# Diagonals from unnormalised taps spread in fp32r, division at the evacuation, and x rows loaded and transposed block by block

## The chip, the cores and the metric

One core of one Trainium2 chip. The metric is the device time of one execution in microseconds, lower is better. The span of a profile is the same execution seen by the profiler, about 1.7 us shorter than the device time.

## The reference, cut to what matters

```python
# x: (8, 4096, 192), weight: (8 heads, 7 taps)
w = softmax(weight, axis=-1)                        # taps of each head
y[b, s, h] = sum_k w[h, k] * x[b, s + k - 6, h]     # causal convolution, zero padded
h = y.reshape(32768, 192) @ w_in                    # w_in: (192, 2048)
g = h * sigmoid(beta * h)                           # beta: one value per column
out = g @ w_out                                     # w_out: (2048, 192), fp32 result
```

## The kernel before

The kernel works on steps of up to 512 tokens of two batch halves at once. One step is 16 units: a unit does six `hidden` matmuls, one ScalarE activation (`Silu(beta*h)`; the factor 1/beta is put into w_out), and the `output` matmuls of the step before. In the steady state VectorE makes the convolved input `ct` two steps ahead, by 21 multiply and multiply-add operations on a transposed `xt`.

The start is different. Step 0 (256 tokens) and step 1 (256 tokens) have no time for that, so TensorE does their convolution with diagonal matrices in fp32r, a cheaper form of fp32 for matmuls (three fp32 matmuls of the taps show as six records in the trace, three fp32r ones as three). The copy of a matmul's result out of PSUM, TensorE's result memory, is called its evacuation. Step 2 is the first whose `ct` VectorE makes. The parts that matter, with cuts:

```python
# w_in chunk 0 is the first load that POOL issues, then sel and ident are built
load_w_in(0)
...                                     # sel (memset, two affine_selects), ident
load_x(nc.gpsimd, x1b, TOK, 0, NB)      # second chunk of x, cast to bf16
for i in range(1, NW): load_w_in(i)
for c in range(0, NF, 4):               # w_out last, four loads
    nc.gpsimd.dma_start(out=w_out_raw[:, c:c+4, :], in_=w_out_v[:, c:c+4, :])
...
nc.scalar.activation(cw8, cw8, AF.Exp, bias=nmax, accum_out=ssum)
nc.vector.reciprocal(rsum, ssum)
nc.vector.tensor_scalar_mul(cw8, cw8, rsum)
fill(6)                                 # matmuls of zeros
for c in range(NG):                     # fp32 spread of the taps to 128 partitions
    nc.tensor.matmul(pc[:, 0, c*K:(c+1)*K], sel[:, c], cw8, start=True, stop=True)
...
transposes(pt, x0b, 0, 0, HB)           # first half of chunk 0
fill(2)
diag_v(1); ...                          # diagonals = ident * taps, fp32r
diag_conv(0, 1, ...)                    # 7 matmuls, then ct by VectorE
diag_conv(0, 2, ...)
transposes(ptb, x0b, HB, 0, HB)         # second half of chunk 0
diag_conv(0, 0, ...)                    # its ct by ScalarE
...
def prep_w_out(c0, n):                  # on POOL, four times, when w_out has landed
    nc.gpsimd.tensor_tensor(w_out_s[:, c0:c0+n, :], w_out_raw[:, c0:c0+n, :],
                            beta_r[:, c0:c0+n].broadcast, ALU.mult)
...
first_work = {                          # extra work inside step 0, by unit
    1: lambda: (more(xt1_work)(), copy_w_in(1)),   # transposes of chunk 1
    3: lambda: (more(xt1_work)(), copy_w_in(2)),
    5: lambda: (more(conv1_work)(), copy_w_in(3)), # taps of step 1, 7 matmuls
    8: more(conv1_work),
    11: more(conv1_work),               # then VectorE evacuates ct of step 1
}
```

`copy_w_in(i)` is a VectorE copy of a w_in chunk from partitions 0-63 to 64-127.

## Time and profile before

| | before |
|---|---|
| device time, median of 3 | 697.0 us (696.14 to 697.85) |
| span of the profile | 695.1 us |
| TensorE busy | 99% |
| first hidden matmul of step 0 | 12.02 us |
| first matmul of step 1 | 25.03 us |
| end of the first hidden group of step 2 | 37.06 us |
| start of the final run of 272 matmuls | 679.63 us |

The last row is a mark near the end: two profiles that differ only in their first 40 us differ at this mark by what the start won or lost.

From the page of the kernel before: the span, busy time by engine, and the chain that ended last.

```profile
span 695.1 us, 24857 instructions
...
PE 686.9 (99%) x11465; PEld 525.9 (76%) x11465; DVE 553.2 (80%) x935; ACT 578.7 (83%) x545; POOL 69.8 (10%) x83
...
PE 96%; DVE 3%; ACT 0%; issue 0%
```

The busy share alone would not prove that TensorE bounds the kernel: the Trainium skill, "Perfetto Trace Analysis", section "Identifying the Most-Contended Engine", says that the matmul busy share is not a good measure of how close a kernel is to roofline, because pipelined TensorE instructions look smaller in the trace. The chain of waits is another road to it, with 96% of the span on TensorE; and after 38 us nothing in the waits view makes TensorE wait longer than 0.2 us. So only the start can move.

The timeline of TensorE at the start (start, duration, engine, line, operation, output<-inputs, shapes, count, and in brackets the idle time before it and what ended it):

```profile
3.94 1.44 PE L208 MATMUL po<-cw_86,sel 8*128 8x7 f32 x6
...
6.87 1.83 PE L249 MATMUL ph<-xt_145,diag 128*128 128x256 f32 x7
...
8.85 1.23 PE L249 MATMUL ph<-xt_145,diag 128*128 128x256 f32 x7
...
10.47 1.09 PE L249 MATMUL po<-xt_145,diag 128*128 128x256 f32 x7
12.02 0.83 PE L363 MATMUL ph<-ct,w_in_s 64*128 64x256 bf16 x12 [0.46 <-ACT ct L261]
...
25.03 0.50 PE L363 MATMUL ph<-ct,w_in_s 64*128 64x256 bf16 x6 [0.54 <-DVE ct L300]
```

The chain of waits from 14 to 37 us (start, duration, what was on it):

```profile
14.88 0.96 DVE xt L314
...
15.87 1.29 DVE w_in_s L149 x2
...
17.18 4.39 DVE ct L344 x3
21.56 2.54 DVE ct L346 x2
24.10 0.87 DVE ct L300
24.97 6.62 DVE ct L346 x10
...
36.67 0.39 PE ph L363 x2
```

After 14.9 us the chain runs on VectorE: the copy of chunk 1's `xt`, two w_in copies, three tap multiplies, two multiply-adds, the evacuation that opens step 1, then the rest of step 2's taps. POOL's w_out multiplications, in POOL's timeline, lie over the middle of it:

```profile
17.00 5.89 POOL L320 TENSOR_TENSOR w_out_s<-w_out_raw,beta_r 128x768 bf16<-128x768 f32 x4 [2.30 <-DMA w_out_raw<-in_moe_w_out_dram]
```

### The profile page before, as it was taken

The page shows a single profiled execution, that of the slowest core. Times are in us where ns is not written, and L with a number is a line of the kernel's source. Part 1 is how long each engine was busy: PE and PEld are TensorE (multiplying, and loading weights), DVE is VectorE, ACT ScalarE, POOL GpSimd, SP SyncE. Part 2 cuts the span into 40 slices and gives each one's busy share as a digit, 9 for nine tenths or more (in the row PEclk, how much of TensorE's full clock was granted, in tenths as well). Part 3 has the DMA queues.
Part 4 walks back from the last instruction along what each step waited for, and adds up shares of the span by engine and source line. Part 5 has one row for each costly group of instructions (what it writes and reads, how often), then busy time and mean ns, then how long its engine had stood idle before and what let it go on. Part 6 is the DMA issues. An engine that isn't in the chain of part 4 may idle for free.

```text
span 695.1 us, 24857 instructions
## 1 busy us (share of the span) xinstructions
PE 686.9 (99%) x11465; PEld 525.9 (76%) x11465; DVE 553.2 (80%) x935; ACT 578.7 (83%) x545; POOL 69.8 (10%) x83
## 2 busy tenths in 40 slices
PE   8899999999999999999999999999999999999997
PEld 6767777777777777777777777777777777777777
DVE  6999999998777987777987777987778987777222
ACT  5898888888888888888888888888888888888881
POOL 6934455000000000000000000000000000000000
PEclk9999999999999999999999999999999999999999
DMA  9999999922232022322023222032123122111012
GB/s 175 146 160 160 169 177 171 138 62 70 54 65 71 27 68 72 47 70 70 26 70 71 49 70 69 26 71 70 48 72 55 41 70 71 48 48 48 25 48 70
DMA packets 181497, 54.57 MB, mean 79 GB/s; under 512 B 146432, under 2 KB 181072, under 8 KB 181392
## 3 DMA queue, kind: packets, MB, share of 16 engines
q0 software_dynamic: 98048, 14.89, 29.9%
q1 hardware_dynamic: 83296, 38.09, 23.6%
q8 instruction: 89, 1.46, 0.9%
q14 instruction: 16, 0.13, 0.1%
q10 hardware_dynamic: 48, 0.01, 0.0%
HBM read 28.98 MB, written 37.29 MB: 95 GB/s over the span
## 4 chain that ended last, share of the span: by engine, by line
PE 96%; DVE 3%; ACT 0%; issue 0%
PE po L410 48%; PE ph L363 46%; DVE ct L346 2%; DVE ct L344 1%; PE ph L204 1%; PE ph L249 0%; PE po L236 0%; PE po L208 0%; DVE w_in_s L149 0%; ACT g L370 0%; PE po L249 0%; DVE xt L314 0%; DVE osb L425 0%; DVE ct L300 0%; DVE osb L424 0%
## 5 line engine op out<-in xcount | busy, mean ns | idle before, releaser
L370 ACT ACTIVATE g<-ph,beta 128x1024 bf16<-128x1024 f32 (+1 forms) x528 | 571.8, 1088 | 97.0 <-PE ph L363 93.1
L410 PEld LDWEIGHTS <-g 64*128 64x128 bf16 x8192 | 368.9, 94 | 102.4 <-issue 0.2
L410 PE MATMUL po<-w_out_s,g 64*128 64x192 bf16 x8192 | 429.8, 243 | 0.0
L363 PE MATMUL ph<-ct,w_in_s 64*128 64x512 bf16 (+1 forms) x3168 | 425.5, 370 | 2.8 <-ACT g L370 1.4
L346 DVE SCALAR_TENSOR_TENSOR ct<-xt,cw,ct 128x512 bf16<-128x512 bf16 x558 | 380.4, 746 | 0.0
L363 PEld LDWEIGHTS <-w_in_s 64*128 64x128 bf16 x3168 | 162.4, 94 | 56.9 <-issue 3.6
L424 DVE COPY osb<-po 128x384 f32<-128x384 f32 x127 | 70.8, 558 | 126.3 <-PE po L410 120.2
L425 DVE TENSOR_TENSOR osb<-po,osb 128x384 f32<-128x384 f32 x129 | 71.5, 554 | 6.0 <-ACT osb L422 1.6
L95 POOL DMA_DIRECT2D xd<-in_x_dram x60 | 54.3, 906 | 47.8 <-DMA xd<-in_x_dram 43.5
L344 DVE TENSOR_SCALAR ct<-xt,cw 128x512 bf16<-128x512 bf16 x93 | 31.6, 393 | 0.0
L422 ACT COPY osb<-po 128x192 f32<-128x192 f32 x2 | 0.6, 318 | 9.9 <-PE po L410 9.9
L320 POOL TENSOR_TENSOR w_out_s<-w_out_raw,beta_r 128x768 bf16<-128x768 f32 x4 | 5.9, 1500 | 2.3 <-DMA w_out_raw<-in_moe_w_out_dram 2.3
L204 PE MATMUL ph<-zeros 128*128 128x512 bf16 x8 | 3.8, 627 | 1.3 <-DVE warm L132 1.3
L249 PE MATMUL po<-xt_145,diag 128*128 128x256 f32 x28 | 4.4, 296 | 0.0
L249 PEld LDWEIGHTS po<-xt_145,diag 128*128 128x128 f32 x28 | 3.6, 189 | 0.7 <-issue 0.6
L149 DVE COPY w_in_s<-w_in_s 64x1536 bf16<-64x1536 bf16 x4 | 2.7, 699 | 1.5 <-DMA w_in_s<-in_moe_w_in_dram 1.4
L184 POOL DMA_DIRECT2D w_out_raw<-in_moe_w_out_dram x4 | 3.1, 782 | 0.0
L249 PEld LDWEIGHTS ph<-xt_145,diag 128*128 128x128 f32 x14 | 2.6, 269 | 0.7 <-ACT xt_145 L270 0.6
L249 PE MATMUL ph<-xt_145,diag 128*128 128x256 f32 x14 | 3.1, 375 | 0.0
L204 PEld LDWEIGHTS <-zeros 128*128 128x128 bf16 x8 | 0.9, 130 | 2.5 <-issue 1.3
L142 POOL DMA_DIRECT2D w_in_s<-in_moe_w_in_dram x4 | 2.6, 667 | 0.8 <-POOLq L479 0.8
L261 ACT CAST ct<-po 128x256 bf16<-128x256 f32 x1 | 0.4, 372 | 2.8 <-PE po L249 2.8
(46 smaller groups left out, 27.7 us busy)
## 6 DMA issues: line engine op xcount, KB each, us to landing
out_dram<-osb SPq DMA_DIRECT2D x60, 384.0 KB, 3.0
xd<-in_x_dram POOLq DMA_DIRECT2D x54, 198.0 KB, 14.6
w_out_raw<-in_moe_w_out_dram POOLq DMA_DIRECT2D x4, 384.0 KB, 9.6
out_dram<-osb SPq DMA_DIRECT2D x7, 192.0 KB, 3.8
xd<-in_x_dram POOLq DMA_DIRECT2D x6, 192.0 KB, 14.0
x_83<-in_x_dram SPq DMA_DIRECT2D x4, 192.0 KB, 3.9
w_in_s<-in_moe_w_in_dram POOLq DMA_DIRECT2D x4, 192.0 KB, 7.9
xt<-xd SPq DMA_TRANSPOSE x30, 4.6
```

The source lines that it names most:

```text
L95: nc.gpsimd.dma_start(out=xd[r0:, :, h, :], in_=x_v[p, t0:t1, h, :].rearrange("t (c d) -> t c d", c=NG),)
L184: nc.gpsimd.dma_start(out=w_out_raw[:, c : c + 4, :], in_=w_out_v[:, c : c + 4, :])
L204: nc.tensor.matmul(pf[:, 0, :], zeros[:, 0:128], zeros, start=True, stop=True)
L249: nc.tensor.matmul(pv, diag[:, c, k, :], xt0[:, c, o : o + n], start=(k == 0), stop=(k == K - 1),)
L320: nc.gpsimd.tensor_tensor(w_out_s[:, c0 : c0 + n, :], w_out_raw[:, c0 : c0 + n, :], beta_r[:, c0 : c0 + n].unsqueeze(2).to_broadcast((128, ...
L344: nc.vector.tensor_scalar_mul(dst, src, scalar)
L346: nc.vector.scalar_tensor_tensor(out=dst, in0=src, scalar=scalar, in1=dst, op0=ALU.mult, op1=ALU.add)
L363: nc.tensor.matmul(ph[:, h, 0:n], w_in_s[rows, j, cols], cts[s][rows, j, 0:n], start=(j == 0), stop=(j == NG - 1),)
L370: nc.scalar.activation(gs[s][:, fc, :, 0:n], ph[:, :, 0:n], AF.Silu, scale=beta[:, fc : fc + 1])
L410: nc.tensor.matmul(po[:, r, b * D : (b + 1) * D], g[rows, fc, h, q * BLK : (q + 1) * BLK], w_out_s[rows, fc, :], start=(fc == 0), stop=(fc ...
L424: nc.vector.tensor_copy(dst, po[:, 0, cols])
L425: nc.vector.tensor_tensor(dst, po[:, 1, cols], dst, ALU.add)
```

## The change

The intent is to start the first hidden matmul earlier. The taps are spread as plain exponentials in fp32r, and the division by their sum moves to the evacuation of the convolution. Only VectorE's own taps are still computed exactly, in fp32, but later, inside step 0. The x rows come in one load per block of 128 tokens, so that transposing starts with the first block, and the second half's transposes move into step 0. POOL builds `sel` and `ident` before it issues w_in. The core, with cuts:

```diff
-    load_w_in(0)                       # was first on POOL, now after sel and ident
+    for b in range(nb):                # one load of x per block, both halves
+        eng.dma_start(out=dst[:, b, :, :], in_=x_v[0, t : t + BLK, :, :])
-    nc.scalar.activation(cw8, cw8, AF.Exp, bias=nmax, accum_out=ssum)
-    nc.vector.reciprocal(rsum, ssum)
-    nc.vector.tensor_scalar_mul(cw8, cw8, rsum)
+    nc.scalar.activation(e8[:, 0:K], cw8, AF.Exp, bias=nmax, accum_out=e8[:, K : K + 1])
-    fill(6)
-    (three fp32 matmuls sel x cw8)
+    nc.vector.tensor_copy(sel_r, sel)           # fp32r copies
+    nc.vector.tensor_copy(e8r, e8)
+    fill(5)
+    spread(pc[:, 0, :], sel_r, e8r)             # three fp32r matmuls
+    fill(1)
...
+    for b in range(HB):                         # cast, transpose, evacuate by block
+        nc.vector.tensor_copy(x0b[:, b], x0[:, b])
+        transposes(pt, x0b, b, 0, 1)
+        nc.scalar.copy(xt0[:, :, HALO + b * BLK : HALO + (b + 1) * BLK], pt)
...
-            nc.scalar.copy(ct[:, c, 0 : steps[s][2]], pv)
+            nc.scalar.mul(ct[:, c, 0:n0], pv, rn[:, c : c + 1])   # the division
...
     first_work = {
-        1: lambda: (more(xt1_work)(), copy_w_in(1)),
-        3: lambda: (more(xt1_work)(), copy_w_in(2)),
-        5: lambda: (more(conv1_work)(), copy_w_in(3)),
+        0: lambda: (first_xt(), taps()),  # second half's transposes; fp32 spread
+        2: lambda: (more(xt1_work)(), copy_w_in(1)),
+        4: lambda: (more(xt1_work)(), copy_w_in(2)),
+        6: lambda: (more(conv1_work)(), copy_w_in(3)),
         8: more(conv1_work),
         11: more(conv1_work),
     }
```

More of the change, by code (lines that the diff above doesn't have):

```diff
@@ L113, with load_x @@
     x1b = setup.tile([128, NB, 2, D], BF16)
-    def load_x(eng, dst, t0, b0, nb):
-        for h in range(2):
-            eng.dma_start(
-                out=dst[:, b0 : b0 + nb, h, :],
-                in_=x_v[0, t0 : t0 + nb * BLK, h, :].rearrange(
-                    "(b q) d -> q b d", q=BLK
-                ),
-            )
+    def load_x(eng, dst, t0, nb):
+        for b in range(nb):
+            t = t0 + b * BLK
+            eng.dma_start(out=dst[:, b, :, :], in_=x_v[0, t : t + BLK, :, :])
+    e8 = setup.tile([H, K + 1], FP32)
     cw8 = setup.tile([H, K], FP32)
     nc.scalar.dma_start(out=cw8, in_=weight)
-    load_x(nc.sync, x0, 0, 0, HB)
-    load_x(nc.sync, x0, HB * BLK, HB, HB)
+    load_x(nc.sync, x0, 0, NB)
     zeros = setup.tile([128, TOK], BF16)
@@ L133 @@
     nc.scalar.activation(warm, warm, AF.Exp)
-    NW = 4
-    FW = F // NW
-    w_in_s = consts.tile([128, NG, F], BF16)
-    def load_w_in(i):
-        cols = slice(i * FW, (i + 1) * FW)
-        nc.gpsimd.dma_start(
-            out=w_in_s[0:DG, :, cols],
-            in_=moe_w_in[:, cols].rearrange("(c d) f -> d c f", c=NG),
-        )
-    def copy_w_in(i):
-        cols = slice(i * FW, (i + 1) * FW)
-        nc.vector.tensor_copy(w_in_s[DG : 2 * DG, :, cols], w_in_s[0:DG, :, cols])
-    load_w_in(0)
     sel = setup.tile([H, NG, 2, DG], FP32)
@@ L177, with load_w_in, copy_w_in @@
     make_identity(nc, ident)
+    NW = 4
+    FW = F // NW
+    w_in_s = consts.tile([128, NG, F], BF16)
+    def load_w_in(i):
+        cols = slice(i * FW, (i + 1) * FW)
+        nc.gpsimd.dma_start(
+            out=w_in_s[0:DG, :, cols],
+            in_=moe_w_in[:, cols].rearrange("(c d) f -> d c f", c=NG),
+        )
+    def copy_w_in(i):
+        cols = slice(i * FW, (i + 1) * FW)
+        nc.vector.tensor_copy(w_in_s[DG : 2 * DG, :, cols], w_in_s[0:DG, :, cols])
+    load_w_in(0)
+    for h in range(2):
+        nc.gpsimd.dma_start(
+            out=x1b[:, :, h, :],
+            in_=x_v[0, TOK : 2 * TOK, h, :].rearrange("(b q) d -> q b d", q=BLK),
+        )
+    for i in range(1, NW):
+        load_w_in(i)
     w_out_raw = setup.tile([128, NF, D], FP32)
     w_out_v = moe_w_out.rearrange("(c p) d -> p c d", p=128)
-    load_x(nc.gpsimd, x1b, TOK, 0, NB)
-    for i in range(1, NW):
-        load_w_in(i)
     for c in range(0, NF, 4):
@@ L190 @@
     nc.vector.reduce_max(nmax, cw8, axis=mybir.AxisListType.X, negate=True)
-    ssum = setup.tile([H, 1], FP32)
-    nc.scalar.activation(cw8, cw8, AF.Exp, bias=nmax, accum_out=ssum)
+    nc.scalar.activation(
+        e8[:, 0:K], cw8, AF.Exp, bias=nmax, accum_out=e8[:, K : K + 1]
+    )
     beta_q = setup.tile([NF, 128], FP32)
@@ L195 @@
     nc.scalar.activation(warm, warm, AF.Silu)
-    rsum = setup.tile([H, 1], FP32)
-    nc.vector.reciprocal(rsum, ssum)
-    nc.vector.tensor_scalar_mul(cw8, cw8, rsum)
+    e8r = setup.tile([H, K + 1], FP32R)
+    sel_r = setup.tile([H, NG, 2, DG], FP32R)
     pc = psum_o.tile([128, 2, TOK], FP32, name="po")
@@ L204, in fill, with spread @@
             nc.tensor.matmul(pf[:, 0, :], zeros[:, 0:128], zeros, start=True, stop=True)
-    fill(6)
-    for c in range(NG):
-        nc.tensor.matmul(
-            pc[:, 0, c * K : (c + 1) * K],
-            sel[:, c, :, :].rearrange("i h d -> i (h d)"),
-            cw8,
-            start=True,
-            stop=True,
-        )
+    def spread(dst, sel, e8):
+        for c in range(NG):
+            nc.tensor.matmul(
+                dst[:, c * (K + 1) : (c + 1) * (K + 1)],
+                sel[:, c, :, :].rearrange("i h d -> i (h d)"),
+                e8,
+                start=True,
+                stop=True,
+            )
+    nc.vector.tensor_copy(sel_r, sel)
     ident_b = setup.tile([128, 128], BF16)
     nc.vector.tensor_copy(ident_b, ident)
-    nc.vector.tensor_copy(x0b[:, 0:HB], x0[:, 0:HB])
-    cw = consts.tile([128, NG, K], FP32)
-    nc.vector.tensor_copy(cw.rearrange("p c k -> p (c k)"), pc[:, 0, 0 : NG * K])
+    nc.vector.tensor_copy(e8r, e8)
+    fill(5)
+    spread(pc[:, 0, :], sel_r, e8r)
+    fill(1)
+    eu = setup.tile([128, NG, K + 1], FP32)
+    nc.vector.tensor_copy(eu.rearrange("p c k -> p (c k)"), pc[:, 0, 0 : NG * (K + 1)])
     diag = setup.tile([128, NG, K, 128], FP32R)
@@ L227, in diag_v @@
             ident.unsqueeze(1).to_broadcast((128, K, 128)),
-            cw[:, c, :].unsqueeze(2).to_broadcast((128, K, 128)),
+            eu[:, c, 0:K].unsqueeze(2).to_broadcast((128, K, 128)),
             ALU.mult,
@@ L255, in diag_tap @@
         )
-    def diag_conv(s, c, pv, ct):
-        for k in range(K):
-            diag_tap(s, c, k, pv)
-        if c == 0:
-            nc.scalar.copy(ct[:, c, 0 : steps[s][2]], pv)
-        else:
-            nc.vector.tensor_copy(ct[:, c, 0 : steps[s][2]], pv)
-    n0 = HB * BLK
-    pt = psum_o.tile([128, NG, n0], BF16, name="po")
-    transposes(pt, x0b, 0, 0, HB)
-    fill(2)
+    n0 = HB * BLK
+    for b in range(HB):
+        nc.vector.tensor_copy(x0b[:, b], x0[:, b])
+        pt = psum_o.tile([128, NG, BLK], BF16, name="po")
+        transposes(pt, x0b, b, 0, 1)
+        nc.scalar.copy(xt0[:, :, HALO + b * BLK : HALO + (b + 1) * BLK], pt)
+    fill(1)
+    diag_v(0)
+    rn = setup.tile([128, NG], FP32)
+    nc.vector.reciprocal(rn, eu[:, :, K])
     diag_v(1)
-    nc.scalar.copy(xt0[:, 0:2, HALO : HALO + n0], pt[:, 0:2, :])
-    nc.vector.tensor_copy(xt0[:, 2, HALO : HALO + n0], pt[:, 2, :])
     for k in range(K):
-        nc.scalar.mul(diag[:, 0, k, :], ident, cw[:, 0, k : k + 1])
-    diag_v(2)
+        nc.scalar.mul(diag[:, 2, k, :], ident, eu[:, 2, k : k + 1])
     ct = ct_pool.tile([128, NG, TOK], BF16, name="ct")
     cts[0] = ct
-    diag_conv(0, 1, psum_h.tile([128, 2, TOK], FP32, name="ph")[:, 0, 0:n0], ct)
-    beta_p = pc[:, 0, 32 : 32 + NF]
-    nc.tensor.transpose(beta_p, beta_q, ident[0:NF, 0:NF])
-    beta = consts.tile([128, NF], FP32)
-    nc.vector.tensor_copy(beta, beta_p)
+    pvs = []
+    for c in range(NG):
+        pool, name = (psum_h, "ph") if c < 2 else (psum_o, "po")
+        pv = pool.tile([128, 2, TOK], FP32, name=name)[:, 0, 0:n0]
+        for k in range(K):
+            diag_tap(0, c, k, pv)
+        if c == 0:
+            nc.vector.tensor_scalar_mul(ct[:, c, 0:n0], pv, rn[:, c : c + 1])
+            copy_w_in(0)
+        elif c == 1:
+            nc.vector.tensor_scalar_mul(ct[:, c, 0:n0], pv, rn[:, c : c + 1])
+            pb = psum_o.tile([128, 2, TOK], FP32, name="po")[:, 0, 0:NF]
+            nc.tensor.transpose(pb, beta_q, ident[0:NF, 0:NF])
+            beta = consts.tile([128, NF], FP32)
+            nc.vector.tensor_copy(beta, pb)
+        else:
+            nc.scalar.mul(ct[:, c, 0:n0], pv, rn[:, c : c + 1])
     beta_r = setup.tile([128, NF], FP32)
@@ L284, with taps, first_xt @@
     nc.vector.tensor_copy(x0b[:, HB:NB], x0[:, HB:NB])
-    copy_w_in(0)
-    diag_conv(0, 2, psum_h.tile([128, 2, TOK], FP32, name="ph")[:, 0, 0:n0], ct)
-    ptb = psum_o.tile([128, NG, n0], BF16, name="po")
-    transposes(ptb, x0b, HB, 0, HB)
-    diag_conv(0, 0, psum_o.tile([128, 2, TOK], FP32, name="po")[:, 0, 0:n0], ct)
-    nc.vector.tensor_copy(xt0[:, :, HALO + n0 :], ptb)
+    cw = consts.tile([128, NG, K], FP32)
+    def taps():
+        pq = psum_o.tile([128, 2, TOK], FP32, name="po")[:, 0, 0 : NG * (K + 1)]
+        spread(pq, sel, e8)
+        pq = pq.rearrange("p (c k) -> p c k", c=NG)
+        rq = setup.tile([128, NG], FP32)
+        nc.vector.reciprocal(rq, pq[:, :, K])
+        nc.vector.tensor_tensor(
+            cw, pq[:, :, 0:K], rq.unsqueeze(2).to_broadcast((128, NG, K)), ALU.mult
+        )
+    def first_xt():
+        pt = psum_o.tile([128, NG, n0], BF16, name="po")
+        transposes(pt, x0b, HB, 0, HB)
+        nc.vector.tensor_copy(xt0[:, :, HALO + n0 :], pt)
     def first_conv():
@@ L299, in first_conv @@
             if c == NG - 1:
-                nc.vector.tensor_copy(cts[1][:, :, 0:n0], pv[:, 0:NG, :])
+                nc.vector.tensor_tensor(
+                    cts[1][:, :, 0:n0],
+                    pv[:, 0:NG, :],
+                    rn.unsqueeze(2).to_broadcast((128, NG, n0)),
+                    ALU.mult,
+                )
             yield
```

## The prediction

> **What bounds the kernel now.** TensorE. The page's busy table gives PE 99% of the 695.1 us span. The waits view after 36 us shows one PE wait of 0.3 us on VectorE, so the steady steps (36.7 us to the end) are matmul-bound and the change does not touch them. Only the first 36.7 us can move.
>
> **The start, from the timeline and the chain of waits.** PE: zero fills 1.27-4.0, fp32 spread of the taps 4.01-5.38 (six passes, 355 ns each), transposes to 6.16, two fills to 7.1, first diagonal taps 7.13, three channels until 11.57, ScalarE evacuation 11.59-11.97, first hidden matmul 12.02. Step 0 runs to 24.5. Then PE waits 0.54 us for the first_conv evacuation, step 1 starts at 25.03, and step 2 at 35.75, with a 0.27 us wait for VectorE at 36.67. From 14.9 to 36.7 the chain is almost all VectorE: transposed x 14.88, w_in copies 15.87-17.16, three tap multiplies 17.18-21.56 at 1.46 us each (393 ns average overall), two multiply-adds, evacuation 24.10-24.97, sixteen multiply-adds. The slow multiplies coincide with POOL's four w_out multiplications (17.0-22.9). The Trainium skill, "SBUF — State Buffer", section "Who interferes with whom", says two-port VectorE operations and GpSimd lock each other out; 1.46 against 1.51 us for the POOL operation agrees. POOL itself waits until 17.0 for the w_out load, and VectorE until 13.5 for the second w_in chunk: this middle is paced by DMA.
>
> **Removed, added, moved.**
> - Spread in fp32r: three short passes instead of six; at most 1.37 us becomes about 0.4 (estimate).
> - Normalisation (reciprocal 0.15 + multiply 0.31) leaves the path to the diagonals; but sel_r and e8r copies join it (about 0.45 and 0.1, estimates from copies of like size). sel is ready 0.8 us earlier, since POOL no longer issues w_in first (0.78).
> - Second-half transposes (0.46) and their 0.95 us copy leave the path to the first hidden matmul.
> - First tap about 6.2 instead of 7.13, the last about 10.3 instead of 11.57, first hidden about 10.7 instead of 12.02: 1.3 us earlier.
> - Added inside step 0: those transposes, an fp32 spread (0.7-1.4), the 0.95 us copy, reciprocal and multiply. That returns 1.2-1.9 us of PE time.
> - The first w_in chunk is issued 2.1 us later and lands about 8.5 instead of 7.0 (issue plus 5.7); it just fits.
>
> **On the critical path.** The later w_in chunks and w_out are issued no earlier, so VectorE's w_in copies (last chunk landing about 15.9) and POOL's 17.0-22.9 block stay. Of the 1.3 us I expect 0-1 us, most likely 0.4-0.6, to survive to the start of step 2.
>
> **Prediction.** 696.5 us, range 695.2 to 697.7. Faster by over 2%: 0.01; within 2%: 0.98; slower by over 2%: 0.01. The gain is below the spread of the runs before (1.7 us).
>
> **What would show it.** First hidden matmul near 10.7; spread under 0.6 us; POOL's w_out block still beginning near 17; tap multiplies still at 1.4 us; step 1 near 24.5 and step 2 near 36.1; the same length from there to the end.
>
> **What would make it wrong.** (1) The PE clock warms later. Taps now go at 225 ns up to about 9.2 us and 149 ns after it; the skill, "TensorE: Matmul & The Clock Gate", Part 1, says the full clock follows a sustained busy window that is free-running. New gaps near 4 and 5 us could delay it and cost up to 1 us. (2) The late w_in chunk makes VectorE's queue wait, delaying the second channel. (3) w_in and w_out land earlier or later than before, moving the VectorE chain with them.

## The result, and the profile after

The changed kernel took 696.64 us, median of 4 runs (696.38 to 696.80), against 696.57 us for the kernel before, median of 4 (696.00 to 697.85). The ratio is 0.9998, with a 95% interval of 0.9981 to 1.0015.

| | before | after |
|---|---|---|
| span of the profile | 695.1 | 695.1 |
| first hidden matmul of step 0 | 12.02 | 10.88 |
| first matmul of step 1 | 25.03 | 25.06 |
| end of the first hidden group of step 2 | 37.06 | 37.08 |
| start of the final run of matmuls | 679.63 | 679.65 |

So the change did what it set out to do, by 1.14 us (12.02 - 10.88), and all of it was gone 14 us later. The page and the timeline of TensorE after:

```profile
span 695.1 us, 24865 instructions
...
PE 687.6 (99%) x11467; PEld 526.6 (76%) x11467; DVE 551.4 (79%) x938; ACT 580.0 (83%) x546; POOL 70.0 (10%) x83
...
PE 96%; DVE 3%; ACT 0%; issue 0%
```

```profile
3.51 0.80 PE L209 MATMUL po<-e8r,sel_r 8*128 8x8 f32 x3
...
6.35 3.36 PE L256 MATMUL ph<-xt_145,diag 128*128 128x256 f32 x14
...
9.85 1.10 PE L256 MATMUL po<-xt_145,diag 128*128 128x256 f32 x7
10.88 0.39 PE L395 MATMUL ph<-ct,w_in_s 64*128 64x256 bf16 x4
11.52 0.28 PE L395 MATMUL ph<-ct,w_in_s 64*128 64x256 bf16 x2 [0.24 <-ACT ct L295]
11.73 0.53 PE L243 MATMUL po<-ident_b,x0b 128*64 128x128 bf16 x12
12.19 0.83 PE L209 MATMUL po<-e_86,sel 8*128 8x8 f32 x6
...
17.54 1.25 PE L395 MATMUL ph<-ct,w_in_s 64*128 64x256 bf16 x12
...
25.06 0.50 PE L395 MATMUL ph<-ct,w_in_s 64*128 64x256 bf16 x6 [0.20 <-ACT g L402]
```

The spread takes 0.80 us instead of 1.44. The first diagonal tap starts at 6.35 instead of 6.87. Two lines then show the bill. The transposes at 11.73 and the fp32 spread at 12.19 are the work that moved out of the way of the first hidden matmul: in the chain of waits they take 0.46 and 0.76 us. They now stand behind hidden group 0 and ahead of hidden group 1. The two hidden groups at 17.54 hold a wait too: they take 1.25 us, where the kernel before takes 0.83 for two groups at 16.62, and the waits view names VectorE's copy of w_in as what TensorE waited for (0.4 us).

The chain of waits after, from 15 to 37 us, and POOL's line:

```profile
15.81 0.96 DVE xt L346
...
16.80 3.05 DVE w_in_s L172 x2
...
19.88 2.92 DVE ct L376 x3
22.79 1.32 DVE ct L378 x2
24.11 0.87 DVE ct L327
24.98 6.62 DVE ct L378 x10
...
36.69 0.39 PE ph L395 x2
```

```profile
16.22 6.16 POOL L352 TENSOR_TENSOR w_out_s<-w_out_raw,beta_r 128x768 bf16<-128x768 f32 x4 [2.48 <-DMA w_out_raw<-in_moe_w_out_dram]
```

The same stations as before are on the chain. The copy of chunk 1's `xt` comes 0.93 us later (15.81 against 14.88), because TensorE reaches chunk 1's transposes later. The two w_in copies take 3.05 us instead of 1.29, the three tap multiplies 2.92 instead of 4.39. The copies of w_in and the tap multiplies that VectorE does during POOL's block are stretched, and the evacuation starts at 24.11 against 24.10.

### The profile page after: what moved, and what is told of

Read it like the earlier page. It is cut to its first block, busy times and chain, and to the rows that moved or that the text cites. A ratio compares the mean times of both kernels' runs of the same rounds, so it can differ in the third digit from the quotient of the medians.

```text
span 695.1 us, 24865 instructions
## 1 busy us (share of the span) xinstructions
PE 687.6 (99%) x11467; PEld 526.6 (76%) x11467; DVE 551.4 (79%) x938; ACT 580.0 (83%) x546; POOL 70.0 (10%) x83
## 3 DMA queue, kind: packets, MB, share of 16 engines
q8 instruction: 89, 1.46, 0.9%
## 4 chain that ended last, share of the span: by engine, by line
PE 96%; DVE 3%; ACT 0%; issue 0%
PE po L442 48%; PE ph L395 46%; DVE ct L378 2%; PE ph L256 0%; DVE w_in_s L172 0%; DVE ct L376 0%; PE ph L205 0%; PE po L209 0%; PE po L243 0%; ACT g L402 0%; PE po L256 0%; DVE xt L346 0%; DVE osb L457 0%; DVE ct L327 0%; ACT xt_145 L269 0%
## 5 line engine op out<-in xcount | busy, mean ns | idle before, releaser
L376 DVE TENSOR_SCALAR ct<-xt,cw 128x512 bf16<-128x512 bf16 x93 | 29.5, 372 | 0.0
L172 DVE COPY w_in_s<-w_in_s 64x1536 bf16<-64x1536 bf16 x4 | 4.4, 1121 | 0.1
```

What stands on the lines that cost most here:

```text
L172: nc.vector.tensor_copy(w_in_s[DG : 2 * DG, :, cols], w_in_s[0:DG, :, cols])
L376: nc.vector.tensor_scalar_mul(dst, src, scalar)
```

## The experiments

Two theories were tested. Theory A: the gain is lost on VectorE, whose chain is locked by POOL's w_out multiplications, and these are paced by a load. Theory B: the work moved into step 0 makes TensorE and ScalarE end step 0 late whatever VectorE does. All results, taken from each run's profile in microseconds (the ratio is to the kernel before, same chip and rounds):

| run | first hidden | step 1 | end of step 2's first group | final run | span | ratio, 95% interval |
|---|---|---|---|---|---|---|
| before | 12.02 | 25.03 | 37.06 | 679.63 | 695.1 | |
| after | 10.88 | 25.06 | 37.08 | 679.65 | 695.1 | 0.9998 (0.9981-1.0015) |
| after_nolock | 10.24 | 24.00 | 35.84 | 678.76 | 694.2 | 0.9997 (0.9982-1.0012) |
| before_nolock | 11.13 | 24.59 | 35.94 | 678.66 | 694.1 | 0.9994 (0.9979-1.0009) |
| after_early_xt | 11.36 | 25.55 | 36.91 | 679.83 | 695.3 | 0.9996 (0.9981-1.0011) |
| after_moved_back | 12.02 | 25.01 | 37.02 | 679.59 | 695.0 | 1.0003 (0.9986-1.0020) |
| after_wout_early | 10.46 | 25.17 | 36.89 | 679.46 | 694.3 | 0.9993 (0.9978-1.0008) |
| before_wout_early | 12.26 | 24.93 | 36.73 | 679.30 | 694.1 | 0.9991 (0.9976-1.0006) |
| after_all_early | 10.07 | 23.74 | 35.70 | 678.27 | 693.1 | 0.9979 (0.9964-0.9994) |
| after_cheap_taps | 10.27 | 24.37 | 36.40 | 678.97 | 694.4 | 0.9997 (0.9980-1.0014) |
| after_balanced | 11.33 | 25.63 | 36.97 | 679.54 | 694.4 | 0.9997 (0.9984-1.0009) |
| after_cheap_early_xt | 10.63 | 24.20 | 36.16 | 678.73 | 694.2 | 0.9999 (0.9985-1.0013) |
| best_more_taps | 10.25 | 25.55 | 38.43 | 681.01 | 695.8 | 1.0006 (0.9991-1.0020) |
| all_early_again | 10.90 | 24.48 | 35.90 | 678.47 | 693.3 | 0.9982 (0.9970-0.9994) |

### The clock is a second variable

Every run that starts from the changed kernel does the same things until the first diagonal tap, at 6.34 or 6.35 us in all eleven profiles. Its first hidden matmul (after_moved_back, which has extra work in front of it, left out) then comes anywhere from 10.07 to 11.36 us. The difference is the TensorE clock. The 14 taps of the first two channels took from 2.60 to 3.36 us; seven taps take 1.5 to 1.6 us at the slow rate and 1.04 at the fast one. In before_nolock all seven of the first channel ran fast from 6.61 us; in after_early_xt and after_balanced all but the last two or three of the 21 ran slow, until about 10.9 us.

The Trainium skill, "TensorE: Matmul & The Clock Gate", Part 1, says that the full clock follows a busy window that is free-running, so that the turning point depends on where the first matmul falls in it. The runs agree that it moves: in the eleven profiles, alike up to the first tap, the taps' pace turned anywhere between about 7.9 and 10.9 us. A single profile's start therefore carries about 1.3 us of luck. A comparison of starts has to look at durations inside step 0 as well as at absolute times. The granted clock in the profile does not show this ramp: the view by stretches reads 1.00 in every one of the first microseconds, while the taps run slow.

### after_moved_back: is the early start worth anything?

```diff
-        0: lambda: (first_xt(), taps()),
+    first_xt(); taps()          # before step 0, ahead of the first hidden matmul
```

> The changed kernel with the second-half transposes and the exact fp32 spread put back ahead of the first hidden matmul. First hidden matmul at about 12.1 instead of 10.88. If those 1.2 us were only relocated (zero sum): step 1 and step 2 start within 0.2 us of the changed kernel (25.06 and 36.69). If the early start had bought something: step 2 starts up to 1.2 us later.

Measured: first hidden matmul at 12.02, which is 1.14 us later than in the changed kernel; step 1 at 25.01 (-0.05), end of step 2's first group at 37.02 (-0.06), final run at 679.59 (-0.06). Its clock turned earlier (14 taps in 2.98 us against 3.36), so that at an equal clock its first hidden matmul would have come about 0.4 us later still; the stations after step 0 agree within 0.06 us all the same. So the early start of the changed kernel bought nothing that this pair of profiles shows, as if the 1.2 us of TensorE work was only relocated. The pair shows it to within those 0.4 us of clock, and it does not tell TensorE's work from VectorE's chain, which passes the same stations in both runs. From the chain of waits of this run:

```profile
15.58 0.96 DVE xt L346
...
16.57 3.23 DVE w_in_s L172 x2
...
19.82 2.91 DVE ct L376 x3
```

The `xt` copy at 15.58 and the stretched w_in copies are those of the changed kernel (15.81, 3.05 us), with the first hidden matmul a whole microsecond later.

### after_nolock and before_nolock: the multiplications taken away

```diff
-            out=w_out_raw[:, c : c + 4, :], in_=w_out_v[:, c : c + 4, :]
+            out=w_out_s[:, c : c + 4, :], in_=w_out_v[:, c : c + 4, :]   # casting load
-    for c in range(0, NF, 4):
-        prep_w_out(c, 4)
```

The result is wrong (the factor 1/beta is missing). The same edit was made to both kernels.

> The changed kernel without POOL's four w_out multiplications (w_out is loaded as bf16 by a casting DMA; the result is wrong on purpose, the factor 1/beta is missing). Theory A (the gain is lost because VectorE's chain is locked by POOL's w_out operations): the two last w_in copies fall from 3.04 us together to about 1.3, the three tap multiplies from 2.92 to about 0.9, VectorE is no longer what step 2 waits for, and step 2 starts about 0.3 us earlier (36.4 instead of 36.7). Theory B (the moved TensorE work makes step 0 longer, so that TensorE and ScalarE together end it late whatever VectorE does): step 1 still starts within 0.3 us of 25.06, and the whole gain stays below 0.5 us.

> The kernel before with the same edit (wrong result on purpose). Theory A alone: both kernels without the lock should keep the 1.1 us lead of the changed kernel, so this one should start step 2 about 1 us later than the changed one without the lock. Theory B: step 1 starts at about 24.5 (hidden of step 0 had ended there), that is 0.4 us BEFORE the changed kernel without the lock, and step 2 at about 35.9.

VectorE's timeline in after_nolock, from the w_in copies to the evacuation:

```profile
16.16 1.51 DVE L172 COPY w_in_s<-w_in_s 64x1536 bf16<-64x1536 bf16 x2
17.70 1.11 DVE L364 TENSOR_SCALAR ct<-xt,cw 128x512 bf16<-128x512 bf16 x3
...
21.54 0.96 DVE L327 TENSOR_TENSOR ct<-po,rn 128x768 bf16<-128x768 f32 x1 [1.40 <-PE po L256]
```

The two copies fell from 3.04 to 1.51 us, the three multiplies from 2.92 to 1.11, and VectorE now waits 1.40 us for TensorE before the evacuation, to which it had come without a wait in the changed kernel. The Trainium skill, "SBUF — State Buffer", section "Who interferes with whom", says that VectorE's two-port operations contend with GpSimd for a shared pair of ports, which whoever issues first holds for the whole instruction while the other is blocked. The runs agree: a tap multiply of 0.29 us (0.87 us for three, undisturbed at 37.59 in the kernel before) took 1.46 us during POOL's block (4.39 us for three), against 1.51 us for one POOL operation.

The final run started 0.89 us earlier than in the changed kernel and 0.97 us earlier than in the kernel before. Of this, the clock gave part: the first hidden matmul came 0.64 and 0.89 us earlier. What belongs to the lock is seen in two places. At step 2 the first hidden group, which spread over 1.50 us in the changed kernel (35.58 to 37.08, waiting for VectorE), took 0.86 us (34.98 to 35.84). And step 0 lasted 13.76 us (10.24 to 24.00) instead of 14.18: the wait for VectorE's copy of w_in is gone from the two hidden groups that took 1.25 us.

```profile
16.90 0.83 PE L383 MATMUL ph<-ct,w_in_s 64*128 64x256 bf16 x12
```

So theory B's mark, step 1 within 0.3 us of 25.06, was missed even with the 0.64 us of clock taken off: the lock held up TensorE's own step 0 by 0.42 us. In the kernel before VectorE's copies had ended at 17.14 us, just after POOL's block began (17.00), and TensorE did not wait for them.

The expectation that before_nolock would start step 1 ahead of after_nolock failed: it started 0.59 us after it. It had met a wait that no theory had listed. TensorE's unit 4 stood until 14.75 us, for a w_in chunk that landed at 13.99. Without the lock the two kernels still finish alike (678.76 and 678.66; medians of 696.17 and 696.03 us). But this pair cannot acquit the lock. Of the lead of 0.89 us in the first hidden matmul, 0.59 was left at step 1, and 0.44 of that is the wait for w_in in before_nolock. In step 1 TensorE then stood for 0.26 us at 31.14 in after_nolock alone, waiting for nothing that the profile shows, and step 1 lasted 10.98 us against 10.52; from the end of step 2's first group to the final run it was 642.92 and 642.72 us, not 642.57. That the two end within 0.1 us is in part chance.

### after_cheap_taps: the added spread taken out

```diff
-        spread(pq, sel, e8)                     # three fp32 matmuls, 0.76 us
-        ...
-        nc.vector.tensor_tensor(cw, pq[:, :, 0:K], rq.broadcast, ALU.mult)
+        nc.vector.tensor_tensor(cw, eu[:, :, 0:K], rn.broadcast, ALU.mult)
```

The taps for VectorE come from the fp32r values; the result was still within tolerance.

> The changed kernel with only the fp32 spread taken out of step 0 (taps for VectorE from the fp32r ones). TensorE reaches the second chunk's transposes 0.76 us earlier. Theory B alone: step 1 starts 0.7 us earlier (24.3). Theory A alone: POOL's multiplications stay at 16.2-22.3, VectorE's evacuation stays within 0.4 us of 24.04 and step 1 gains at most 0.4 us.

Measured: step 1 at 24.37, 0.69 us earlier, with a start that was 0.61 us earlier by the clock. TensorE had ended step 0 at 23.3, as theory B wanted, but then stood for VectorE:

```profile
22.24 1.08 PE L390 MATMUL ph<-ct,w_in_s 64*128 64x256 bf16 x12 [0.45 <-ACT g L397]
24.37 0.50 PE L390 MATMUL ph<-ct,w_in_s 64*128 64x256 bf16 x6 [1.04 <-DVE ct L322]
```

This is the plainest sign that two limits lie almost on top of each other. In the changed kernel TensorE ends step 0 at 24.86 and waits 0.20 us for ScalarE, until 25.06, and VectorE's evacuation ends at 24.98. Bring the first forward, by the 0.76 us of the spread and the 0.61 us of clock, and a wait of 1.04 us for the second appears. Both theories are half right: step 1 came where theory B had it, but with the clock's help, and theory A's mark was missed, since VectorE's evacuation came at 23.37, 0.67 us earlier and not within 0.4 us of 24.04 (POOL's block began at 15.80).

### after_early_xt: chunk 1's transposes back at units 1 and 3

```diff
-        0: lambda: (first_xt(), taps()),
-        2: lambda: (more(xt1_work)(), copy_w_in(1)),
-        4: lambda: (more(xt1_work)(), copy_w_in(2)),
-        6: lambda: (more(conv1_work)(), copy_w_in(3)),
+        0: first_xt,
+        1: lambda: (more(xt1_work)(), copy_w_in(1)),
+        3: lambda: (more(xt1_work)(), copy_w_in(2)),
+        4: taps,
+        5: lambda: (more(conv1_work)(), copy_w_in(3)),
```

> The changed kernel with the transposes of the second chunk back at units 1 and 3 and the exact taps moved to unit 4 (first_xt stays at unit 0). If the later order of these transposes is what delayed VectorE's chain: the x copy on VectorE moves from 15.81 to about 14.6 and the evacuation that lets step 1 start moves forward by up to 0.9 us. If POOL's lock sets the pace instead (theory A): the copy moves but the evacuation stays within 0.3 us of 24.04. Total within 0.5 us of the changed kernel either way.

The copy moved from 15.81 to 14.95, although this run had the slowest clock of all (first hidden at 11.36). VectorE's evacuation began at 23.72 instead of 24.04, 0.32 us earlier: at the edge of what theory A allowed, and well short of the 0.86 us by which the copy had moved. Step 1 began late, at 25.55, because step 0 had begun late; step 0 lasted 14.19 us (11.36 to 25.55) against 14.18 (10.88 to 25.06). The order of the transposes moved VectorE and took nothing off step 0; what it spared VectorE shows only at step 2, whose first group no longer waited (0.84 us instead of 1.50).

### after_wout_early and before_wout_early: w_out through another queue

```diff
-        nc.gpsimd.dma_start(out=w_out_raw[:, c : c + 4, :], in_=...)
+    nc.vector.memset(w_out_raw[:, :, 0:1], 0.0)       # holds the load back to 7 us
+        nc.sync.dma_start(out=w_out_raw[:, c : c + 4, :], in_=...)
```

> The changed kernel, correct result, with w_out loaded through SP's queue from about 7 us (after a one-column memset that VectorE reaches then) instead of last through POOL's queue. If the lock with POOL's w_out multiplications sets the pace (theory A): those start by about 13 instead of 16.22 and are done by about 18-19, mostly while VectorE would wait anyway; the last w_in copies and the tap multiplies get shorter, VectorE stops being what step 2 waits for, and step 2's first two hidden groups end 0.5 to 1.3 us earlier than 37.08 (the run without the multiplications ended that group about 1.2 us earlier, of which 0.64 came from an earlier clock). If w_in chunks come later because w_out shares the DMA engines, the gain is lost to that wait.

> The kernel before with the same early w_out load. If the changed kernel's early start is worth something once the lock is gone, this one starts step 2 later than the changed one with early w_out by about the lead in the first hidden matmul (up to 1.1 us, less the 1.2 us of work moved into step 0: so about 0). Theory B expects within 0.3 us of each other.

The expectation failed: POOL's first multiplication began at 16.32, not near 13.

```profile
16.32 1.47 POOL L353 TENSOR_TENSOR w_out_s<-w_out_raw,beta_r 128x768 bf16<-128x768 f32 x1 [7.17 <-DMA w_out_raw<-in_moe_w_out_dram]
19.52 5.38 POOL L353 TENSOR_TENSOR w_out_s<-w_out_raw,beta_r 128x768 bf16<-128x768 f32 x3 [1.74 <-DMA w_out_raw<-in_moe_w_out_dram]
```

POOL waited 7.17 us for the load. In the changed kernel POOL had issued w_out at 7.24 us, so "early" was a misreading of mine: the issue time hardly moved, only the queue did. The Trainium skill, "Trainium Kernel Development and Optimization", section "Key Constraints", says that all queues run on the same 16 DMA engines and interleave, so that another issuing engine saves only issue time. The run agrees: 16.32 against 16.22. The other three multiplications even moved back, to 19.52 and later, and the lock fell on the multiply-adds (3.83 us for two instead of 1.40). TensorE also stood 0.67 us for VectorE's copy of w_in, at 17.72.

As expected, the two kernels with this edit ended alike (679.46 and 679.30), although one began its first hidden matmul 1.80 us before the other.

The edit did one thing that nobody had expected. In the five kernels with it (six profiles, one kernel having been run twice), the end of the span follows the start of the final run of matmuls by 14.8 or 14.9 us. In the eight profiles without it that time is 15.4 or 15.5 us. The last store lands equally fast in the changed kernel and in after_all_early (1.6 us at the least). The difference comes after that landing. The records of SyncE's sequencer in the packed traces, which the views leave out, show nine waits on semaphores that SyncE passes one after the other before it ends. In all eight profiles without the edit the wait for the last store is the second of them, and from its landing SyncE needs 0.85 to 0.87 us for the other seven; in all six with the edit it is the sixth, five have been passed while the store was under way, and the other three take 0.25 us. Why the edit reorders these waits was not looked into.

### after_all_early, all_early_again and after_cheap_early_xt: the edits together

after_all_early has the edits of after_wout_early, after_early_xt and after_cheap_taps. after_cheap_early_xt has the last two. all_early_again is after_all_early run once more.

> The changed kernel with early w_out, the second chunk's transposes at units 1 and 3, and the taps for VectorE taken from the unnormalised fp32r ones by one VectorE multiply, so no fp32 spread (0.76 us of TensorE) in step 0. Correct within tolerance. If both limits named so far (lock, and TensorE work moved into step 0) are the whole of it: step 0 lasts about 13.3 us instead of 14.2 and the group of step 2 named above ends 1.2 to 2 us before 37.08; total 0.1 to 0.3% below both kernels.

> The changed kernel with the cheap taps and the early transposes but w_out loaded as in the changed kernel. If w_out's early load is not what helped the all-early version (its first multiplication began at 16.29 against 16.22, so the load landed no earlier): the final run of matmuls begins within 0.5 us of 678.3, apart from the clock's phase, and the end of the span follows it by 15.4 us as in the changed kernel, not 14.8. If it did help: it begins near 679.

> The all-early version, unchanged, a second time. If its 0.21% was a gain of the kernel: 0.1 to 0.25% below the kernel before again. If it was the clock's phase (its profiled run had the earliest full clock of all with this start): within 0.1% of the kernel before. The end of the span follows the start of the final run of matmuls by 14.8 us, as in the other runs with w_out on SP's queue.

after_all_early was the first version with an interval clear of 1: 694.90 us median against 696.67, ratio 0.9979. Its repetition with five rounds gave 695.02 against 696.30, ratio 0.9982 (0.9970 to 0.9994). The result was correct. The repetition had the late clock (first hidden matmul at 10.90, practically that of the changed kernel), and step 0 lasted 13.58 us (10.90 to 24.48) against 14.18: so at the same clock the rearranged step 0 saves 0.6 us. The first hidden group of step 2, which waits for VectorE, took 0.91 us instead of 1.50, another 0.6. Together that is the 1.18 us of the final run (678.47 against 679.65), and the 0.6 us at the end come on top: a third of what the profile gained (693.3 against 695.1) is not a gain at the start.

after_cheap_early_xt, without the w_out edit, started its final run at 678.73, within the expected half microsecond, and its end followed 15.5 us later as expected. Its timing did not separate it from the kernel before, though (0.9999): its profiled execution took 695.89 us, while two others of the same kernel took 696.86 and 697.01. So one profile is not enough to credit it with the microsecond that its marks show.

### after_balanced: spreading the diagonal taps

```diff
+            if i % 2 == 1 and i < NG * K - 2:
+                yield                 # two taps per unit, units 3 to 12
+    first_work = {u: more(conv1_work) for u in range(3, 13)}
```

> The changed kernel with the last run's edits (early w_out on SP, taps from the fp32r ones) and the other TensorE work of step 0 spread evenly: second chunk's transposes at units 1 and 2, the 21 taps of the first chunk's second half two per unit from unit 3 to 12 instead of seven at 6, 8 and 11, and one more VectorE operation ahead of the evacuation. If step 0 is held up by TensorE blocks of 1.05 us that starve ScalarE (0.76 to 0.79 us idle three times in the last run but one): those waits shrink below 0.3 us each and step 1 starts 1 to 1.5 us after where VectorE's evacuation allows, about 22.5 against 23.74. VectorE should then be what step 2 waits for: the first group of step 2 ends near 34.5 against 35.7. Total 694 us, 0.3% below the kernel before. If VectorE's chain is the limit from the start, the gain over the all-early version is under 0.4 us.

Besides this cut, the run has the edits of after_wout_early and after_cheap_taps, chunk 1's transposes at units 1 and 2, and one more tap operation of VectorE ahead of the evacuation.

ScalarE's waits of 0.76 to 0.79 us did shrink, to 0.18, and yet step 1 began only at 25.63. Taps in bursts of seven had taken 0.15 us each at the full clock (1.04 for seven). In pairs between hidden groups they cost about 0.22 us each, 0.43 per unit, so TensorE became the slower of the two engines:

```profile
16.57 0.50 PE L252 MATMUL po<-xt,diag 128*128 128x256 f32 x2
17.01 0.50 PE L392 MATMUL ph<-ct,w_in_s 64*128 64x256 bf16 x6
17.44 0.51 PE L252 MATMUL po<-xt,diag 128*128 128x256 f32 x2
```

Each unit now takes 0.87 us (16.57 to 17.44). TensorE ended step 0 at about 24.97 us and then waited 0.65 us for VectorE. The run also had a late clock, with nearly all of the first 21 taps slow. The expected 694 us became 696.07.

### best_more_taps: more of VectorE's work ahead of the evacuation

```diff
-    pops = {1: 12, 2: 26}
+    pops = {1: 10, 2: 26}
-            ... if s else u > 5
+            ... if s else (u > 5) + (u in (9, 10))
```

> The all-early version with two more of VectorE's tap operations ahead of the evacuation that opens step 1 (VectorE waited 1.53 us for TensorE there). If VectorE's chain is what step 2 waits for: the 0.27 us wait and the stretched first group of step 2 (1.44 us from its first matmul to its last, against 0.65 without a wait) go away and the run gains 0.5 to 0.8 us over the all-early version at an equal clock phase. If the clock is late in this run, first hidden matmul near 11.3 instead of 10.1, up to 1.3 us of that are hidden.

This one lost, 1.0006, with executions from 695.14 to 698.12. Here POOL's block ran into the added operations (four multiply-adds took 5.23 us), the evacuation came at 24.55 (21.29 and 22.51 in the two runs of the all-early version), and TensorE stood still for 1.93 us. What that cost is more than the wait:

```profile
22.54 1.08 PE L391 MATMUL ph<-ct,w_in_s 64*128 64x256 bf16 x12 [0.45 <-ACT g L398]
25.55 0.82 PE L391 MATMUL ph<-ct,w_in_s 64*128 64x256 bf16 x6 [1.93 <-DVE ct L323]
...
26.80 0.85 PE L391 MATMUL ph<-ct,w_in_s 64*128 64x256 bf16 x6
...
29.08 0.49 PE L391 MATMUL ph<-ct,w_in_s 64*128 64x256 bf16 x6
```

A hidden group of six took 0.82 us and more until 28.7, then 0.49 again. The view by stretches shows why; its last columns are the granted clock, the DMA share and GB/s:

```profile
24.00:25.50 1.50, 0.00 (x0) 0.00 (x0) 1.50 (x3) 0.35 (x1) 1.50 (x3) 0.95 0.72 154
25.50:27.00 1.50, 1.45 (x16) 1.21 (x18) 1.50 (x3) 0.59 (x1) 1.50 (x3) 0.50 1.92 206
27.00:29.00 2.00, 2.00 (x30) 1.66 (x26) 2.00 (x4) 0.83 (x3) 2.00 (x4) 0.56 2.39 156
29.00:31.00 2.00, 2.00 (x48) 1.89 (x45) 2.00 (x4) 2.00 (x4) 2.00 (x3) 1.00 2.34 146
```

The clock was halved after the idle time and came back about three microseconds later. The wait on VectorE of 1.93 us cost TensorE about another 1.5 us in matmuls (half of the time from 25.55 to 28.7). Step 2 no longer waited for VectorE, as intended, but by then its first group ended at 38.43: the evacuation that TensorE needs for step 1 had stood behind the added work in the same queue.

## Why the prediction was right or wrong

The time was right: 696.64 us measured, 696.5 predicted, inside 695.2 to 697.7 and within 2%. This says little of the mechanism, since a change that did nothing would have fitted as well (696.57 for the kernel before). The step-by-step forecast was right in its main mechanism and wrong in how much would survive.

- **Only the first 36.7 us can move.** Right for this change: from the end of step 2's first group to the final run it is 642.57 us in both profiles (679.63 - 37.06 and 679.65 - 37.08).
- **First hidden matmul 1.3 us earlier, at about 10.7.** Nearly right: 10.88, 1.14 us earlier. The terms were off in part. The spread took 0.73 us on the chain, not "about 0.4", and the last tap ended at about 10.96, not 10.3. The second is warning (1) of the prediction come true: the 14 taps of the first two channels ran at the slow rate (3.36 us). The eleven profiles show that this is chance as much as the change.
- **1.2 to 1.9 us of TensorE work come back inside step 0.** Right, at the low end: 0.46 + 0.76 = 1.22 us. Add the 0.24 us wait for the third channel's evacuation, take off 0.34 us because step 1's last wait shrank from 0.54 to 0.20, and one has 1.12 of the 1.17 us by which step 0 grew (14.18 against 13.01).
- **"Of the 1.3 us I expect 0-1 us, most likely 0.4-0.6, to survive to the start of step 2."** The centre of this failed in the two profiles: nothing survived, 36.69 against 36.67, and step 1 came at 25.06, not near 24.5. The prediction had counted the returned work and then still credited a gain, though lead (1.14) and return (1.22) cancel; after_moved_back agrees, to within 0.4 us. What would survive at an equal clock is not shown. The taps' pace turned at about 9.9 us in the changed kernel and 9.2 in the kernel before, and half of this difference, some 0.3 us, is an estimate of what that cost; the timings (0.9981 to 1.0015) cannot tell so little.
- **"POOL's 17.0-22.9 block stay[s]", "tap multiplies still at 1.4 us".** Wrong in detail, and so was the reason given, that the later loads "are issued no earlier": POOL issued the later w_in chunks at 5.37 us instead of 6.03 and w_out at 7.24 instead of 7.89. The block came at 16.22, and fell on the w_in copies (1.29 to 3.05 us) more than on the multiplies (4.39 to 2.92). The sum that VectorE loses hardly changed: copies and multiplies together took 5.68 us before (1.29 + 4.39) and 5.97 after. The nolock runs show the lock as a cost of both kernels. In the changed one it also held up TensorE inside step 0, by 0.42 us, and these runs do not settle how much of the lead was lost to it.
- **The late first w_in chunk "just fits".** Right: VectorE copied it at 8.77 without a wait in the profile.

What is not shown: how much of the 1.14 us each part of the change contributed (read from the traces only), how the loss divides between the returned work and the lock, what would survive at an equal clock, and why the closing waits come in another order with w_out on SP's queue.

## What to carry to other kernels

Work taken out of the way of the first useful matmul has to go somewhere; if it stays on the same engine inside a stage which that engine paces, the lead is spent there, so find the station where the two traces meet again before believing an earlier start. When two chains end about a tenth of a microsecond apart, shortening one only uncovers the wait on the other: here the spread, the order of transposes and the load's queue each bought no measurable time alone, while together they gave 0.2%, a third of it at the end of the program (without the queue, the other two gave 0.9999). And look at more than one profile before crediting a microsecond at the start, because the clock's turning point alone moved it by 1.3 us.

## What the Trainium skill lacked or had wrong

- "TensorE: Matmul & The Clock Gate", Part 1, places the turn to the full clock around 4 us into sustained matmuls, within about 0.5 us from run to run. Here, with zero matmuls from 1.26 us on, it came at about 4.7 us in one profile (before_nolock, where the records of the spread come 0.21 us apart and then 0.11) and only at about 10.9 us in two: from 3.4 to 9.6 us after the first matmul.
- The same page and part has the clock fall back after an idle window of about 3.4 us, and its closing table warns of idle gaps above about 3 us. In best_more_taps, in the one profile of it, an idle time of 1.93 us was followed by a granted clock of 0.50 and hidden groups of 0.82 us instead of 0.49 for three microseconds. After an idle time of 1.04 us (after_cheap_taps) the granted clock stayed at 1.00.
- I found no page with the cost of fp32r matmuls that change their weights every time: 0.15 us each for 128x128 weights and 256 columns in bursts of seven, about 0.22 us each in pairs between bf16 groups.
- I found no page that says that the order of SyncE's closing waits counts: from the last store's landing they took 0.86 us where its wait was the second of nine, and 0.25 us where it was the sixth (four loads moved from POOL's queue to SP's).
